# Filter network laid out by feature: VectorE takes relu times decay out of PSUM, no transposes; weights' lower part in one operation, scalars packed

## The chip, the cores and the metric

The kernel runs on one core of one Trainium2 chip. The metric is device time in microseconds (us) of one execution; the median of three runs of the kernel before is 2228.44 us (2227.22 to 2228.93). The five engines work in parallel, each through its own list of instructions in order: TensorE (PE, with its weight loads as PEld), VectorE (DVE), ScalarE (ACT), GpSimd (POOL) and SyncE (SP). SP, ACT and POOL can also issue transfers (DMA); this kernel's loads go out from SP's queue, a few from ACT's. A transfer is carried out by up to 16 DMA engines.

## The reference, cut to what matters

```python
# pos_emb (12480, 64), w1 (64, 64), w2 (64, 128), x and v (2, 12480, 128)
h_mlp = np.maximum(pos_emb @ w1, 0.0) @ w2          # the filter network
window = np.exp(-0.01 * pos)[:, None]               # the decay, positive
h_filt = h_mlp * window
y = irfft(rfft(x * v, 2*S) * rfft(h_filt, 2*S))[:, :S]
x = (x * y).reshape(-1, 128)
h = x @ w_in                                         # w_in (128, 2048), w_out (2048, 128), both float64
g = (a0 + a1*h + a2*h*h + a3*h**3) / (1 + |b0|*|h| + |b1|*h*h + 1e-6)
out = g @ w_out
```

Because the decay is positive, it may stand before the relu, after it, or on the product. In float32 it is zero from position 10398 on, so only the first 82 of 98 blocks of 128 positions carry a filter.

## The kernel before, in words

A position is 128 m + t. The kernel runs in three stretches.

**The first stage** (the loop `for i in range(nb + 2)`, 16 steps of work) computes the filter and prepares weights. A step takes four pairs of residues t, 82 blocks m each, so 328 columns. `load_pos` fetches four rows of `pos_emb` for each m on both sides of the middle (SP, L276, tile `pos`); `hf_w` multiplies them with the decay (DVE, L480 and L486, tile `pw`); `hf_t` turns them to feature-major by four PE transposes (L500) that ACT copies out of PSUM (L503); `hf_1` multiplies with `w1`, placed twice on the diagonal of `bdw1` (PE, L507), and ACT takes the relu out of PSUM (L509, tile `zu`); `hf_2` multiplies with `w2` (PE, L515), and ACT copies the result into `hf` (L521).

Beside it, `weights_gen` turns the float64 words of `w_in` and `w_out` into float32, in 16 pieces of 128 x 256 through tile `raw` (L317, L319). One step of it: DVE takes the two words apart with shifts and masks (L330 to L338) and combines them (L339, tile `f`); POOL adds the two parts (L341); one step later DVE clears what is too small (L346) and ACT scales and rounds (L459, L460 into `win_h`, or L463 into `wout`); a further step later POOL computes the lower part of `w_in` (L455, `win_l`). The steps before the loop's `i = 5` have none of it; 13 pieces are begun in this stage.

Also beside it, POOL multiplies the first 8 of 32 pieces of x and v (L245, `hu`, loaded by L237 and L238 with two buffers each), and DVE computes the scalars of the activation from `a` and `b` in chains of 128 x 1 operations (L361, L364 and others).

**The second stage** (`for g in range(NG + 3)`) does the convolution of the first batch in 32 groups; its first DVE instruction is L563. Each iteration ends with one more x times v on DVE, 24 times, and after those with a remaining step of `weights_gen`.

**The second part** does everything else (second batch, activation, both weight multiplications) and takes most of the time. It comes behind a branch on a computed flag.

All engines follow the order in which the code is written. SP too works in order: a load that waits for a buffer holds up the loads written behind it.

Of the kernel before, what the change touches and what calls it, by code (L numbers as in the profile page):

```python
# [9 lines left out]
F32 = mybir.dt.float32  # L10
# [11 lines left out]
M = 98  # L22
# [40 lines left out]

def constants():
# [31 lines left out]
    win = win.reshape(M, N2)[:96]  # L96
# [14 lines left out]
def build(ctx: ExitStack, tc, x, x_q, v_q, pos_emb, w1, w2, w_in, w_out, moe_a, moe_b,  # L111
# [145 lines left out]
    with ExitStack() as st:  # L257
# [4 lines left out]
        win, bdw1, bdw2 = flat[0][0:96, 0:N2], flat[1][:, 0:128], flat[2][:, 0:2 * D]  # L262
# [5 lines left out]
        NPL = 4  # L268
        pos_t = {}

        def load_pos(p0):
            t = sp.tile([M, 2 * NPL, FO], F32, tag="wa", name="pos", bufs=3)
            for o, t0 in ((0, H2 + p0), (NPL, H2 - p0 - NPL)):
                if MF < M:
                    for r0, r1 in ((0, MF // 16 * 16), (MF // 16 * 16, MF)):
                        nc.sync.dma_start(out=t[r0:r1, o:o + NPL], in_=rows(pos_emb, r0, r1 - r0, t0, NPL, 0, FO))  # L276
                else:
                    load_rows(t[:, o:o + NPL], pos_emb, t0, NPL, 0, FO, True)
            pos_t[p0] = t

        load_pos(0)
        nc.sync.dma_start(out=win, in_=win_d)
        nc.sync.dma_start(out=ident, in_=ident_d)
        load_pos(NPL)
# [38 lines left out]
        def to_f32(raw, n):  # L323
# [4 lines left out]
            fa = sp.tile([128, n], F32, tag="f", name="f", bufs=2)  # L328
# [29 lines left out]

        def ts(o, i, s1, op0, s2=None, op1=None):
            kw = {} if op1 is None else {"op1": op1}  # L360
            nc.vector.tensor_scalar(out=col(o), in0=col(i), scalar1=s1, scalar2=s2, op0=op0, **kw)  # L361

        def tt(o, i, j, op):
            nc.vector.tensor_tensor(out=col(o), in0=col(i), in1=col(j), op=op)  # L364

        def scalars():


            for i in range(4):
                col(f"a{i}")  # L370
            for i in range(2):
                col(f"b{i}")
            nc.scalar.dma_start(out=sc[:, 0:4], in_=moe_a.unsqueeze(0).to_broadcast([128, 4]))
            nc.scalar.dma_start(out=sc[:, 4:6], in_=moe_b.unsqueeze(0).to_broadcast([128, 2]))
            for n in ("a0", "a1", "a2", "a3", "b0", "b1"):
                nc.scalar.activation(out=col("m" + n), in_=col(n), func=AF.Abs)
            tt("sum", "ma0", "ma1", ALU.add)
            tt("sum", "sum", "ma2", ALU.add)
            tt("sum", "sum", "ma3", ALU.add)
            yield  # L380

            ts("d", "ma3", 1e-30, ALU.max)
            nc.vector.reciprocal(out=col("d"), in_=col("d"))
            tt("q", "ma2", "d", ALU.mult)
            tt("q", "q", "ma2", ALU.mult)
            ts("lim", "sum", 16.0, ALU.mult)
            tt("flag", "q", "lim", ALU.is_le)
            ts("q", "ma3", 1024.0, ALU.mult)
            tt("q", "q", "sum", ALU.is_ge)
            yield  # L390
            tt("flag", "flag", "q", ALU.mult)
            ts("q", "mb1", 1e-9, ALU.is_ge)
            tt("flag", "flag", "q", ALU.mult)
            ts("q", "mb1", 1e9, ALU.is_le)
            tt("flag", "flag", "q", ALU.mult)
            tt("q", "mb0", "mb0", ALU.mult)
            ts("lim", "mb1", 16.0, ALU.mult)
            tt("q", "q", "lim", ALU.is_le)
            tt("flag", "flag", "q", ALU.mult)
            yield  # L400
            ts("not", "flag", -1.0, ALU.mult, 1.0, ALU.add)

            tt("b1e", "mb1", "flag", ALU.mult)
            tt("b1e", "b1e", "not", ALU.add)
            tt("a3e", "a3", "flag", ALU.mult)
            tt("a3e", "a3e", "not", ALU.add)
            yield

            for o, i in (("eta", "b1e"), ("sb1", "mb1")):
                ts("d", i, 1e-30, ALU.max)  # L410
                nc.scalar.activation(out=col("d"), in_=col("d"), func=AF.Ln)
                nc.scalar.activation(out=col(o), in_=col("d"), func=AF.Exp, scale=0.5)
                for _ in range(2):
                    nc.vector.reciprocal(out=col("d"), in_=col(o))
                    tt("d", "d", i, ALU.mult)
                    tt("d", "d", o, ALU.add)
                    ts(o, "d", 0.5, ALU.mult)
                yield
# [25 lines left out]
        def weights_gen():  # L444
# [663 lines left out]
```

## Time and profile before

| what | value |
|---|---|
| median of three runs | 2228.44 us |
| the profiled execution's own time | 2228.3 us |
| its span, first to last instruction | 2226.4 us |
| first stage | 0 to 78.6 us |
| second stage | 78.6 to about 357 us |
| DVE busy in the span | 2060.4 us (93%) |
| POOL busy | 2014.7 us (90%) |
| PE busy | 1951.9 us (88%) |
| ACT busy | 1932.1 us (87%) |

Rows of a timeline give start, duration, engine, line, operation, the tiles written and read, and in brackets how long the engine had been idle before and what released it. A line of a helper stands for all who call it. The profiled execution lies within the three runs.

### The profile page before, as it was taken

What the parts mean: (1) busy time and instruction counts of PE and PEld (TensorE: products, weight loads), DVE (VectorE), ACT (ScalarE), POOL (GpSimd) and SP (SyncE); (2) the same over time, 40 slices, a digit from 0 to 9 for tenths busy, and PEclk for the clock granted to TensorE, in tenths of its full rate; (3) what the DMA queues carried; (4) which work ended last, traced back from release to release, by engine and by line L of the source; (5) the groups of instructions that cost most, each with busy time, mean ns of one, the idle gap of its engine ahead of it and who ended that gap; (6) DMA issues with size and microseconds to landing.
All of it is one profiled execution on the core that took longest, in us unless ns stands there. A gap on an engine that the chain in (4) does not pass through costs nothing.

```text
span 2226.4 us, 25191 instructions
## 1 busy us (share of the span) xinstructions
PE 1951.9 (88%) x8352; PEld 1307.8 (59%) x8352; DVE 2060.4 (93%) x2322; ACT 1932.1 (87%) x1971; POOL 2014.7 (90%) x1605
## 2 busy tenths in 40 slices
PE   6899987899999999999999788888888888888886
PEld 4678766566666666666666455445545545545543
DVE  7899995899999998999999889999999999999997
ACT  6422214999999999999999999999999999999997
POOL 5477755999999999999999789999999999999998
PEclk9999988999999999999999999999999999999999
DMA  5344324433143233222222212221122111121100
GB/s 161 108 138 151 120 75 137 118 95 77 39 108 91 51 81 88 74 63 74 56 65 53 49 32 47 48 48 33 31 46 39 38 40 33 48 48 33 36 10 10
DMA packets 148283, 149.61 MB, mean 67 GB/s; under 512 B 88766, under 2 KB 117824, under 8 KB 145264
## 3 DMA queue, kind: packets, MB, share of 16 engines
q1 hardware_dynamic: 141120, 124.16, 22.1%
q10 hardware_dynamic: 7024, 23.76, 3.3%
q8 instruction: 68, 1.11, 0.2%
q14 instruction: 71, 0.58, 0.1%
HBM read 99.72 MB, written 48.17 MB: 66 GB/s over the span
## 4 chain that ended last, share of the span: by engine, by line
POOL 37%; ACT 36%; DVE 10%; PE 9%; issue 5%; DMA 2%; SPq 0%; POOLq 0%; DVEq 0%; ACTq 0%
POOL v L983 18%; POOL v L977 8%; ACT v L912 8%; ACT r L961 8%; ACT l L956 7%; ACT q L940 6%; ACT q L888 5%; POOL q L951 4%; POOL q L950 2%; PE cs L155 2%; PE cs L582 2%; DVE q L967 2%; DVE q L972 1%; ACT q L945 1%; DVE v L922 1%
## 5 line engine op out<-in xcount | busy, mean ns | idle before, releaser
L983 POOL TENSOR_TENSOR v<-v,q 128x970 f32<-128x970 f32 (+3 forms) x416 | 936.3, 2252 | 42.5 <-DVE q L972 40.9
L992 PE MATMUL acc<-v,wout 128*128 128x485 f32 (+3 forms) x1664 | 765.9, 583 | 123.9 <-POOL v L983 116.9
L922 DVE SCALAR_TENSOR_TENSOR v<-v,sc,h 128x970 f32<-128x970 f32 (+3 forms) x416 | 502.9, 1209 | 36.7 <-ACT q L888 32.3
L967 DVE SCALAR_TENSOR_TENSOR q<-q,sc,r 128x970 f32<-128x970 f32 (+3 forms) x416 | 502.6, 1208 | 36.9 <-ACT r L961 34.0
L992 PEld LDWEIGHTS acc<-v,wout 128*128 128x128 f32 x1664 | 293.8, 192 | 377.3 <-POOL v L983 185.0
L972 DVE SCALAR_TENSOR_TENSOR q<-q,r 128x970 f32<-128x970 f32 (+3 forms) x416 | 480.1, 1154 | 13.4
L912 ACT ACTIVATE v<-h,sc 128x970 f32<-128x970 f32 (+3 forms) x416 | 445.3, 1105 | 19.5 <-PE h L880 19.2
L961 ACT ACTIVATE r<-l 128x970 f32<-128x970 f32 (+3 forms) x416 | 426.0, 1024 | 8.7 <-DVE q L972 7.9
L878 PE MATMUL h<-ahi,win_l 128*128 128x486 f32 (+3 forms) x832 | 391.7, 471 | 47.2 <-DVE v L922 45.4
L977 POOL TENSOR_SCALAR v<-v,sc 128x980 f32<-128x980 f32 (+6 forms) x321 | 420.8, 1311 | 0.1
L956 ACT ACTIVATE l<-q,sc 128x1940 f32<-128x1940 f32 (+3 forms) x208 | 405.3, 1949 | 2.2 <-POOL q L951 2.1
L879 PE MATMUL h<-alo,win_h 128*128 128x486 f32 (+3 forms) x832 | 319.3, 384 | 0.0
L888 ACT ACTIVATE q<-h 128x970 f32<-128x970 f32 (+3 forms) x303 | 311.4, 1028 | 8.4 <-PE h L880 8.3
L880 PE MATMUL h<-ahi,win_h 128*128 128x486 f32 (+3 forms) x832 | 317.9, 382 | 0.0
L878 PEld LDWEIGHTS h<-ahi,win_l 128*128 128x128 f32 x832 | 158.2, 190 | 175.7 <-DVE v L922 109.6
L940 ACT ACTIVATE q<-q,sc 128x1940 f32<-128x1940 f32 (+2 forms) x95 | 189.8, 1998 | 0.0
L879 PEld LDWEIGHTS h<-alo,win_h 128*128 128x128 f32 x832 | 158.8, 191 | 35.0 <-issue 19.9
L880 PEld LDWEIGHTS h<-ahi,win_h 128*128 128x128 f32 x832 | 158.3, 190 | 25.7
L945 ACT ACTIVATE q<-q,sc 128x1470 f32<-128x1470 f32 (+3 forms) x113 | 170.9, 1512 | 0.0
L820 PEld LDWEIGHTS cv<-yc,gt 90*98 90x98 f32 x1004 | 118.8, 164 | 31.7 <-DVE an L826 14.4
L820 PE MATMUL cv<-yc,gt 90*98 90x128 f32 x1004 | 128.1, 274 | 7.0 <-DVE an L826 5.6
L951 POOL TENSOR_TENSOR q<-q 128x490 f32<-128x490 f32 (+3 forms) x113 | 111.0, 982 | 9.4
(112 smaller groups left out, 2622.8 us busy)
## 6 DMA issues: line engine op xcount, KB each, us to landing
yc<-y_d SPq DMA_DIRECT2D x23, 900.0 KB
gt<-in_g_dram SPq DMA_DIRECT2D x48, 344.5 KB
xq<-in_x_q_dram SPq DMA_DIRECT2D x64, 196.0 KB
vq<-in_v_q_dram SPq DMA_DIRECT2D x64, 196.0 KB
h_d<-hg ACTq DMA_DIRECT2D x32, 360.0 KB
y_d<-ys ACTq DMA_DIRECT2D x16, 720.0 KB
hg<-h_d SPq DMA_DIRECT2D x64, 180.0 KB
y_d<-ys SPq DMA_DIRECT2D x16, 720.0 KB
```

Of the source, the lines that this page charges most:

```text
L878: nc.tensor.matmul(out=t[:, k, 0:w], lhsT=wl, rhs=hi[:, 0:w], start=True, stop=False)
L879: nc.tensor.matmul(out=t[:, k, 0:w], lhsT=wh, rhs=lo[:, 0:w], start=False, stop=False)
L880: nc.tensor.matmul(out=t[:, k, 0:w], lhsT=wh, rhs=hi[:, 0:w], start=False, stop=True)
L912: nc.scalar.activation(out=v, in_=st_h[s, i], func=AF.Square, bias=col("s"))
L922: stt(out=v, in0=v, scalar=col("k"), in1=h, op0=ALU.add, op1=ALU.mult)
L956: nc.scalar.activation(out=part(st_l, s, i), in_=part(st_q, s, i), func=AF.Ln, **({"bias": col("ka")} if short else {}))
L961: nc.scalar.activation(out=t[:, :, 0:w], in_=halves(st_l[s], i, w), func=AF.Exp, scale=-1.0)
L967: nc.vector.scalar_tensor_tensor(out=q, in0=q, scalar=col("ka") if short else 0.0, in1=st_r[s, i], op0=ALU.add, op1=ALU.mult)
L972: nc.vector.scalar_tensor_tensor(out=q, in0=q, scalar=2.0, in1=st_r.pop((s, i)), op0=ALU.subtract, op1=ALU.mult)
L977: nc.gpsimd.tensor_scalar(out=v, in0=v, scalar1=col("p0" if short else "a0"), scalar2=1.0, op0=ALU.add, op1=ALU.mult)
L983: nc.gpsimd.tensor_tensor(out=v, in0=v, in1=halves(st_q[s], i, w), op=ALU.mult)
L992: nc.tensor.matmul(out=acc[j][:, 0:w], lhsT=wout[:, f, :], rhs=st_v[s][:, i, 0:w], start=(f == 0), stop=(f == NF - 1), skip_group_check=True)
```

## The change

The filter network is laid out by feature. The host passes `pos_q`, in which each step's 128 x 328 input is already feature-major (64 features of the one side of the middle, 64 of the other), so the loads, the multiplication by the decay on DVE and the transposes with their ACT copies go. The decay comes as a second tile of 128 x 328 per step, `win`: two rows of 328 numbers, each of them read for 64 partitions. DVE takes relu times decay out of PSUM in one operation in place of ACT's relu. The unpacking of weights has one operation fewer; the lower part of `w_in` is one DVE operation that also scales, so POOL's subtraction and one of ACT's two operations go; tile `f` has three buffers. The scalars take 39 small DVE operations in place of 65, and their two loads stand first in ACT's queue. `weights_gen` starts at `i = 3` in place of 5, so 14 pieces are begun in the first stage. The identity is loaded late.

```diff
+def by_pair(a):
+    a = np.moveaxis(a[:MF], (0, 1), (-1, -2))
+    a = np.stack([a[..., H2:, :], a[..., H2 - 1::-1, :]])
+    return np.moveaxis(a.reshape(a.shape[:-2] + (H2 // NP, NP * MF)), -2, 0)
...
-        def load_pos(p0):
-            t = sp.tile([M, 2 * NPL, FO], F32, tag="wa", name="pos", bufs=3)
-            for o, t0 in ((0, H2 + p0), (NPL, H2 - p0 - NPL)):
-                if MF < M:
-                    for r0, r1 in ((0, MF // 16 * 16), (MF // 16 * 16, MF)):
-                        nc.sync.dma_start(out=t[r0:r1, o:o + NPL], in_=rows(pos_emb, r0, r1 - r0, t0, NPL, 0, FO))
...
+        def load_pos(i):
+            if i < nb:
+                t = sp.tile([128, W], F32, tag="wa", name="pos", bufs=3)
+                w = sp.tile([128, W], F32, tag="wn", name="win", bufs=3)
+                nc.sync.dma_start(out=t, in_=pos_q[i])
+                nc.sync.dma_start(out=w, in_=win_d[i].unsqueeze(1).to_broadcast([2, FO, W]))
+                pos_t[i] = (t, w)
+
+        nc.scalar.dma_start(out=sc[:, 0:4], in_=moe_a.unsqueeze(0).to_broadcast([128, 4]))
+        nc.scalar.dma_start(out=sc[:, 4:6], in_=moe_b.unsqueeze(0).to_broadcast([128, 2]))
         load_pos(0)
...
+        load_pos(1)
+        load_pos(2)
...
-            fa = sp.tile([128, n], F32, tag="f", name="f", bufs=2)
+            fa = sp.tile([128, n], F32, tag="f", name="f", bufs=3)
...
-            V.tensor_scalar(out=ib, in0=hi, scalar1=signed(0xC0000000), scalar2=None, op0=ALU.bitwise_and)
...
-            V.tensor_tensor(out=ia, in0=ia, in1=ib, op=ALU.bitwise_or)
+            V.scalar_tensor_tensor(out=ia, in0=hi, scalar=signed(0xC0000000), in1=ia, op0=ALU.bitwise_and,
+                                   op1=ALU.bitwise_or)
...
-                        nc.gpsimd.tensor_tensor(out=win_l[:, o], in0=t, in1=win_h[:, o].bitcast(F32), op=ALU.subtract)
+                        nc.vector.scalar_tensor_tensor(out=win_l[:, o], in0=t, scalar=col("eta"),
+                                                       in1=win_h[:, o].bitcast(F32), op0=ALU.mult, op1=ALU.subtract)
...
-                        nc.scalar.activation(out=t, in_=t, func=AF.Identity, scale=col("eta"))
-                        nc.scalar.activation(out=win_h[:, (k - 1) * WN:k * WN], in_=t, func=AF.Identity)
+                        nc.scalar.activation(out=win_h[:, (k - 1) * WN:k * WN], in_=t, func=AF.Identity,
+                                             scale=col("eta"))
...
+        def hf_1(i):
+            t, w = pos_t.pop(i)
             ps = cvs()
+            nc.tensor.matmul(out=ps[:, 1, 0:W], lhsT=bdw1, rhs=t, start=True, stop=True)
             rT[i] = ctile(sp, "zu", 2, CG).rearrange("p r c k -> p (r c k)")[:, 0:W]
-            nc.scalar.activation(out=rT[i], in_=ps[:, 1, 0:W], func=AF.Relu)
+            nc.vector.scalar_tensor_tensor(out=rT[i], in0=ps[:, 1, 0:W], scalar=0.0, in1=w, op0=ALU.max, op1=ALU.mult)
+            load_pos(i + 3)
...
-            for _ in range(2):
-                next(sg, None)
-            if i >= 5:
+            next(sg, None)
+            if i >= 3:
                 next(wg, None)
```

**On DVE, one late step of the first stage** (`pw` is the product with the decay, `raw` the float64 words, `f` and `i_` the unpacking's tiles). Before:

```order
L480 TENSOR_TENSOR pw<-pos,ta_85 82x4x64
L486 TENSOR_TENSOR pw<-pos,ta_85 82x4x64
L346 SCALAR_TENSOR_TENSOR f<-i_634,f 128x256
L330 TENSOR_SCALAR i_678<-raw 128x256
L332 TENSOR_SCALAR i_679<-raw 128x256
L333 TENSOR_SCALAR i_680<-raw 128x256
L335 TENSOR_TENSOR i_678<-i_678,i_679 128x256
L336 TENSOR_SCALAR i_681<-raw 128x256
L338 TENSOR_SCALAR i_679<-i_678 128x256
L339 SCALAR_TENSOR_TENSOR f<-i_680,i_679 128x256
```

and with the change, where `zu` is relu times decay, `cs` PSUM and `win` the decay's tile:

```order
L461 SCALAR_TENSOR_TENSOR zu<-cs,win 128x328
L435 SCALAR_TENSOR_TENSOR win_l<-f,sc,win_h 128x256
L353 SCALAR_TENSOR_TENSOR f<-i_475,f 128x256
L337 TENSOR_SCALAR i_506<-raw 128x256
L339 TENSOR_SCALAR i_508<-raw 128x256
L341 SCALAR_TENSOR_TENSOR i_506<-raw,i_506 128x256
L343 TENSOR_SCALAR i_509<-raw 128x256
L345 TENSOR_SCALAR i_507<-i_506 128x256
L346 SCALAR_TENSOR_TENSOR f<-i_508,i_507 128x256
```

The two products with the decay and one unpacking operation are gone; relu times decay and the lower part have come to DVE.

**On SP, the loads of one step** while x and v are still being loaded. Before:

```order
L317 DMA raw<-in_moe_w_in_dram 128x512
L237 DMA xq<-in_x_q_dram 98x512
L238 DMA vq<-in_v_q_dram 98x512
L276 DMA pos<-in_pos_emb_dram 80x256
L276 DMA pos<-in_pos_emb_dram 2x256
L276 DMA pos<-in_pos_emb_dram 80x256
L276 DMA pos<-in_pos_emb_dram 2x256
```

and with the change:

```order
L324 DMA raw<-in_moe_w_in_dram 128x512
L244 DMA xq<-in_x_q_dram 98x512
L245 DMA vq<-in_v_q_dram 98x512
L283 DMA pos<-in_pos_q_dram 128x328
L284 DMA win<-in_win_dram 128x1x328
```

Four loads of `pos_emb` rows have become one of `pos_q` and one of the decay, in the same place behind x and v; the size printed is that of the tile written, the source of the last one being 2 x 64 x 328.

## Rows read from the trace of the kernel before

**Rows 1.** The page: busy us, share of the span and instructions of each engine.
```profile
PE 1951.9 (88%) x8352; PEld 1307.8 (59%) x8352; DVE 2060.4 (93%) x2322; ACT 1932.1 (87%) x1971; POOL 2014.7 (90%) x1605
```

**Rows 2.** Stretches: window, length, busy PE, PEld, DVE, ACT, POOL, clock, DMA share, GB/s.
```profile
0.00:20.00 20.00, 9.61 (x38) 6.09 (x38) 10.15 (x44) 6.19 (x18) 4.21 (x8) 1.00 0.57 166
...
120.00:140.00 20.00, 20.00 (x110) 16.05 (x109) 19.72 (x29) 5.32 (x10) 16.74 (x17) 1.00 0.54 168
```

**Rows 3.** Timeline of one late step of the first stage, POOL and DVE.
```profile
61.49 0.83 POOL L341 TENSOR_TENSOR f<-f,i 128x256 f32<-128x256 f32 x1 [0.54 <-DVE f L339]
...
61.66 0.94 DVE L486 TENSOR_TENSOR pw<-pos,ta 82x256 f32<-82x256 f32 x1
62.29 2.59 POOL L455 TENSOR_TENSOR win_l<-f,win_h 128x256 fp32r<-128x256 f32 x1
...
64.92 0.42 DVE L339 SCALAR_TENSOR_TENSOR f<-i,i 128x256 f32<-128x256 int32 x1 [0.62 <-POOL win_l L455]
...
65.42 0.83 POOL L341 TENSOR_TENSOR f<-f,i 128x256 f32<-128x256 f32 x1 [0.54 <-DVE f L339]
```

**Rows 4.** Timeline of DVE over the last steps, up to the second stage.
```profile
70.12 0.43 DVE L346 SCALAR_TENSOR_TENSOR f<-i,f 128x256 f32<-128x256 int32 x1 [0.84 <-POOL f L341]
...
73.25 0.43 DVE L346 SCALAR_TENSOR_TENSOR f<-i,f 128x256 f32<-128x256 int32 x1 [0.84 <-POOL f L341]
...
78.27 0.43 DVE L339 SCALAR_TENSOR_TENSOR f<-i,i 128x256 f32<-128x256 int32 x1
78.62 0.90 DVE L563 TENSOR_TENSOR tb<-cs,twh 128x720 f32<-128x720 f32 x1
```

**Rows 5.** Timeline of POOL where it still multiplies x and v.
```profile
31.14 0.84 POOL L341 TENSOR_TENSOR f<-f,i 128x256 f32<-128x256 f32 x1 [6.62 <-DVE f L339]
...
35.44 0.84 POOL L341 TENSOR_TENSOR f<-f,i 128x256 f32<-128x256 f32 x1 [0.36 <-DVE f L339]
```

**Rows 6.** Timeline of DVE at the start.
```profile
7.01 0.22 DVE L547 TENSOR_SCALAR tb<-tb 64x128 f32<-64x128 f32 x1
...
29.18 0.28 DVE L330 TENSOR_SCALAR i<-raw 128x256 int32<-128x256 int32 x1
```

**Rows 7.** Groups by line, 0 to 150 us: count, busy us, mean ns of one.
```profile
L364 DVE TENSOR_TENSOR sc<-sc 128x1 f32<-128x1 f32 x39 | 7.9, 209 | 2.8 <-ACT sc L376 1.7
...
L346 DVE SCALAR_TENSOR_TENSOR f<-i,f 128x256 f32<-128x256 int32 x12 | 5.0, 414 | 2.5 <-POOL f L341 2.5
...
L361 DVE TENSOR_SCALAR sc<-sc 128x1 f32<-128x1 f32 x18 | 2.7, 152 | 0.6
```

**Rows 8.** DMA, 89.5 to 95 us: packets, MB, engines' share; loads in it.
```profile
q1 hardware_dynamic: 224, 0.40, 29.3%
q10 hardware_dynamic: 144, 0.37, 17.8%
...
h_d<-hg ACTq DMA_DIRECT2D x1, 360.0 KB
xq<-in_x_q_dram SPq DMA_DIRECT2D x1, 196.0 KB
vq<-in_v_q_dram SPq DMA_DIRECT2D x1, 196.0 KB
```

**Rows 9.** DMA, 12 to 16 us: the same columns.
```profile
q1 hardware_dynamic: 666, 1.00, 85.3%
```

**Rows 10.** DMA, 0 to 4 us: busy share of the 16 engines in 40 slices.
```profile
DMA  0000000000000000028745222596511355532558
```

**Rows 11.** Timeline of DVE late in the second stage.
```profile
283.33 0.49 DVE L346 SCALAR_TENSOR_TENSOR f<-i,f 128x256 f32<-128x256 int32 x1
...
289.27 0.90 DVE L563 TENSOR_TENSOR tb<-cs,twh 128x720 f32<-128x720 f32 x1
...
320.13 0.91 DVE L563 TENSOR_TENSOR tb<-cs,twh 128x720 f32<-128x720 f32 x1 [0.52 <-POOL zu L180]
...
327.95 0.91 DVE L563 TENSOR_TENSOR tb<-cs,twh 128x720 f32<-128x720 f32 x1 [0.51 <-POOL zu L180]
```

More of the change, by code (lines that the diff above doesn't have):

```diff
@@ L95, in constants @@
     win[:S] = WINDOW
-    win = win.reshape(M, N2)[:96]
+    win = by_pair(win.reshape(M, N2))
     return {
@@ L261, in build @@
         flat = [sp.tile([128, CG * 2 * K1], F32, tag=t, name=t + "0", bufs=2) for t in ("ta", "ta", "tb")]
-        win, bdw1, bdw2 = flat[0][0:96, 0:N2], flat[1][:, 0:128], flat[2][:, 0:2 * D]
+        bdw1, bdw2 = flat[1][:, 0:128], flat[2][:, 0:2 * D]
         twh = sp.tile([N2, 2, 2 * K1], F32, name="twh")
@@ L366, in scalars @@
         def scalars():
[L369 to L377, printed above, removed]
@@ L391, in scalars @@
[L391 to L403, printed above, removed]
@@ L404, in scalars @@
[L404 to L412, printed above, removed]
-                for _ in range(2):
[L414 to L418, printed above, removed]
@@ L431, in scalars @@
[L431 to L442 removed]
+            V = nc.vector
@@ new lines, in scalars @@
+            mul, add, le, ge = ALU.mult, ALU.add, ALU.is_le, ALU.is_ge
+            nc.scalar.activation(out=cols("ma0", "mb1"), in_=cols("a0", "b1"), func=AF.Abs)
+            ts("sum", "ma0", "ma1", add, "ma2", add)
+            ts("lim", "sum", "ma3", add, 16.0, mul)
+            ts("sum", "sum", "ma3", add)
+            ts("d", "ma3", 1e-30, ALU.max)
+            V.reciprocal(out=col("d"), in_=col("d"))
+            ts("q", "ma3", 1024.0, mul, "sum", ge)
+            ts("d", "d", "ma2", mul, "ma2", mul)
@@ new lines, in scalars @@
+            ts("flag", "d", "lim", le, "q", mul)
+            ts("lim", "mb1", 16.0, mul)
+            ts("q", "mb0", "mb0", mul, "lim", le)
+            ts("flag", "mb1", 1e-9, ge, "flag", mul)
+            ts("flag", "mb1", 1e9, le, "flag", mul)
+            ts("flag", "flag", "q", mul)
+            ts("not", "flag", -1.0, mul, 1.0, add)
+            ts("b1e", "mb1", "flag", mul, "not", add)
+            ts("a3e", "a3", "flag", mul, "not", add)
+            i, o, d = cols("mb1", "b1e"), cols("sb1", "eta"), sc[:, 30:32]
@@ new lines, in scalars @@
+            V.tensor_scalar(out=d, in0=i, scalar1=1e-30, scalar2=None, op0=ALU.max)
+            nc.scalar.activation(out=d, in_=d, func=AF.Ln)
+            nc.scalar.activation(out=o, in_=d, func=AF.Exp, scale=0.5)
+            yield
+            for _ in range(2):
+                V.reciprocal(out=d, in_=o)
+                V.tensor_tensor(out=d, in0=d, in1=i, op=mul)
+                V.tensor_tensor(out=d, in0=d, in1=o, op=add)
+                V.tensor_scalar(out=o, in0=d, scalar1=0.5, scalar2=None, op0=mul)
@@ new lines, in scalars @@
+            V.reciprocal(out=cols("ie", "i3"), in_=cols("eta", "a3e"))
+            ts("s", "a2", "eta", mul, "i3", mul)
+            ts("s", "s", 0.5, mul)
+            ts("k", "a1", "b1e", mul, "i3", mul)
+            ts("q", "s", "s", mul)
+            ts("k", "k", "q", ALU.subtract)
+            ts("p0", "a0", "eta", mul, "b1e", mul)
+            ts("p0", "p0", "i3", mul)
+            yield
+            ts("wf", "a3e", "ie", mul, "ie", mul)
+            ts("wf", "wf", "ie", mul, -1.0, mul)
@@ L529, in build @@
         load_u()
-        load_u()
-        for i in range(nb + 2):
+        nc.vector.tensor_scalar(out=bdw2[64:128, D:], in0=bdw2[64:128, D:], scalar1=-1.0, scalar2=None, op0=ALU.mult)
+        for i in range(nb + 1):
             if i < nb:
-                hf_t(i)
-            if 0 <= i - 1 < nb:
-                hf_1(i - 1)
-            if 0 <= i - 2 < nb:
-                hf_2(i - 2)
-            if i == 12:
+                hf_1(i)
+            if i >= 1:
+                hf_2(i - 1)
+            if i == 11:
                 nc.sync.dma_start(out=f1, in_=f1_d)
@@ L545, in build @@
                 nc.sync.dma_start(out=idfth, in_=idfth_d)
-            if i == 0:
-                nc.vector.tensor_scalar(out=bdw2[64:128, D:], in0=bdw2[64:128, D:], scalar1=-1.0, scalar2=None, op0=ALU.mult)
-            for _ in range(2):
-                next(sg, None)
-            if i >= 5:
+                nc.sync.dma_start(out=ident, in_=ident_d)
+            next(sg, None)
+            if i >= 3:
                 next(wg, None)
@@ L1093 @@
     feeds = [("x", inputs["x"]), ("x_q", by_quarter(inputs["x"])), ("v_q", by_quarter(inputs["v"]))]
-    feeds += [(n, inputs[n]) for n in _INS[2:]] + list(constants().items())
+    feeds += [("pos_q", by_feature(inputs["pos_emb"]))] + [(n, inputs[n]) for n in _INS[3:]] + list(constants().items())
     for name, a in feeds:
```

96 lines of the change are left out of this document (19 added, 77 removed).

## The prediction, written before the changed kernel had run

> **What bounds the kernel now.** I began with the page: DVE, POOL, PE and ACT are all busy 87 to 93% [rows 1], which says little, since the change touches only the first 78.6 us and a little of the second stage. So I read the stretches next, then the timeline.
>
> In the first 20 us no engine is busy for more than half the time [rows 2]: the stage starts with waits. DVE does its scalars between the steps, and the first piece of weights is taken up at 29.18 us [rows 6]. From there the pace is that of `weights_gen`. While x and v are multiplied, one addition of POOL follows the other after 4.30 us, 31.14 to 35.44 [rows 5]. Later it is 3.93 us, 61.49 to 65.42 [rows 3]. There the reader is to see a circle: DVE's L339 at 64.92 waits for POOL's `win_l`, whose 2.59 us are long only because DVE works beside it, and POOL's next addition waits for L339. When no `win_l` is left, a step takes 3.13 us, 70.12 to 73.25, of which DVE idles 0.84 us for POOL's addition [rows 4]. DVE then enters the second stage at 78.62 us [rows 4], and there it is the bound: 19.72 us of 20 [rows 2]. What the first stage gains or loses up to 78.62 therefore goes through to the end, since all behind it hangs on DVE's order.
>
> DMA is not the bound now: 166 GB/s at a share of 0.57 [rows 2], with peaks at 85% [rows 9].
>
> **DVE and POOL, if all loads were there in time.** First relu: `bdw2` is scaled at 7.01 us [rows 6]; its load goes out two issues later now, so I put 7.9 us. 39 small operations follow at 0.19 us (between 152 and 209 ns [rows 7]), 7.4 us, and four relus. One relu reads 328 numbers from PSUM. Before shows no such operation; between 414 ns for 256 numbers [rows 7] and 0.90 us for 720 out of PSUM [rows 4] lies 0.49 us, or some 0.42 from start to start. With 0.2 us for ACT's logarithm and exponential the first piece is taken up at 7.9 + 7.4 + 1.7 + 0.2 = 17.2 us, where before had 29.18.
>
> Then 13 steps. Five beside POOL's x times v take 4.3 us each as now (one operation less on DVE, `win_l` more). Four with `win_l` on DVE take 3.2 us, four without it 2.94: the 3.13 us less one operation of 0.2 us, the relu lying in the 0.84 us that DVE idles, since a product that reads PSUM does not stand still for POOL (0.90 us each in the second stage with POOL at work [rows 11]). `win_l` reads two tiles in SBUF, as L486 does, whose 0.94 us beside POOL's addition [rows 3] stand for a wait; hence 3.2 and not 2.9. Sum: 17.2 + 1.35 + 5 x 4.3 + 4 x 3.2 + 4 x 2.94 + 0.35 = 65.0 us to the second stage, 13.6 us early. PE and ACT have less to do than now, and each step leaves them time: ACT four copies and one rounding, PE two products and eight small ones.
>
> **The loads.** Here I expect the other sign. In 89.5 to 95 us three loads ran: x and v, each 98 rows of 2 KB (196 KB), and one transfer of 128 rows (360 KB) on ACT's queue [rows 8]. Queue 1 shows 224 packets. 196 are the rows; 28 are left, 14 for each load. Queue 10 shows 144, that is 128 and 16. I read the extra packets as one closing packet for each DMA engine that took part: 98 rows are dealt to 14 engines, 128 to 16, the largest number up to 16 by which the count divides. The code before cuts 82 rows into 80 and 2, which fits.
>
> The decay's load has a source of 2 rows, each read 64 times, and a target of 128 partitions. The trace has no load whose two sides begin with different counts. If the target's count decides, it goes to 16 engines; if both must divide, to 2. I take 2, since a share of the work has to be a share of both sides' outer counts, and these have only 2 in common. The Trainium skill, page "DMA: Bandwidth & Descriptors", section "Why a DMA increments its semaphore by 16 and not by 1", says that the engines used are the largest number up to 16 that divides the slowest counts of both sides, and that they are the lowest-numbered ones; the extra packets above agree for equal counts, and no row here shows unequal ones. By that rule the load takes 2 engines, always the same two, and the sum is the one that follows; without it, it would be the first rival's.
>
> I further assume that it is always the same two. On two engines each window load is 64 packets of 1312 bytes, 84 KB, on each of them. And since every other load of SP's queue also has a part on these two, behind whatever was issued before, all loads of the stage come at the pace of these two. Up to the last of the 16 windows each carries 16 x 84 KB = 1.344 MB of decay, 16 x 8 x 1312 bytes = 0.168 MB of `pos`, 20 loads of x and v with 7 rows of 2 KB = 0.287 MB, 11 pieces of `raw` with 16 KB = 0.180 MB, and 0.025 MB of constants: 2.00 MB.
>
> What does one engine move? In 12 to 16 us, all crowded, 1.00 MB took 85.3% of 16 engines [rows 9], 54.6 us of engine time: 18.3 GB/s. The quiet transfer of queue 10 took 17.8% of 16 engines over 5.5 us, 15.7 us for 0.37 MB [rows 8]: 23.6 GB/s. The two engines will not share with fourteen busy ones, so I go near the upper, 22 GB/s; 18.3 and 23.6 are the ends. 2.00 MB then take 91.0 us (109.3; 84.7). Bytes begin to move at 1.7 us [rows 10], so the last window lands at 92.7 us. Does the queue run dry? No: three windows are ahead, each 3.8 us on the two engines, and SP is held up behind x and v only for a multiplication of POOL.
>
> Behind the last window still stand: its next piece of `raw` 0.7 us, taking it up 1.35, two more steps of 2.94, 0.35 to the second stage, together 8.3 us. Second stage at 101.0 us: 22.4 us late. Most of DVE's work of 65.0 us lies inside the waits and counts no more.
>
> **The second stage.** An iteration with a step of weights took from 283.33 to 289.27 us on top of the rest; 5.94 us, against which a plain iteration of 7.82 (320.13 to 327.95) has 0.52 us of idling [rows 11], so 5.3 us in all. One of three such steps now lies in the first stage: 5.3 us less. The remaining two have one operation fewer: 0.5 us. Together 5.8 us (5 to 7).
>
> **Sum.** 22.4 - 5.8 = 16.6 us more. From the profiled execution's 2228.3 us, which is the median within 0.2, that makes 2245 us. With 23.6 GB/s and 7 us it is 2237, with 18.3 GB/s and 5 us 2264.
>
> **The rivals.**
> - The window load goes to 16 engines, or to two that change from load to load, so that windows travel side by side. Then a step's loads (336 KB of `pos` and `win`, 262 KB of `raw`, 401 KB of x and v: 1.0 MB) take 4.0 us at the 250 GB/s of [rows 9] (1.00 MB in 4 us) against a step of 4.3, DVE and POOL set the pace, and 13.6 + 5.8 us are gained: 2209 us. For it: the target has 128 rows, and all large loads here use 14 or 16. Against it: the source's count. It decides if a window load is closed by 16 packets, or if two windows land close together.
> - Two engines, but quick enough to be hidden. No change needs the second stage at 84.4 us, so 2.00 MB in 74.4 us, 26.9 GB/s each; no row shows that. It would give 2228 us.
> - Two engines, and slower than the crowded ones, as in the short bursts of queue 1 in [rows 8]: 29.3% of 16 engines over 5.5 us, 25.8 us for 0.40 MB, 15.5 GB/s. 2.00 MB take 129 us, the time is 2283 us.
> - A smaller gain: loads in time, but DVE and POOL stay in step at 3.9 us as now, because `win_l` on DVE stands still for POOL: 8 steps x 0.85 = 6.8 us less gain, 2216 us.
>
> A rule that speaks on the last one stands in the Trainium skill, page "SBUF — State Buffer", section "Who interferes with whom": a DVE operation with two SBUF inputs and a POOL operation that reads SBUF exclude each other for a whole operation, and one with at most one SBUF input does not contend. L486's 0.94 us agree. By it `win_l` waits and the relu does not, as priced above, and the sum stays.
>
> **How the numbers follow.** Forecast 0.80, 16 engines with the full gain 0.09, smaller gain 0.03, hidden 0.04, slower than crowded 0.04. The time is the forecast's, 2245 us; the range takes its own ends, 2236 to 2264, and leaves out some 0.2. Runs of this kernel lie within 0.1% of each other, and 0.2%, 4.5 us, is about what tells a change from none: faster 0.13, same 0.04, slower 0.83.
>
> **What would show it.** Right: in the first stage DVE stands before the relu for `win` and before the unpacking for `raw`; a window comes about every 5 to 6 us; the share of the DMA engines stays low while loads are outstanding; first product with `twh` near 101 us; two steps of weights in the second stage. Wrong: first product near 65 us and DVE hardly waiting for loads; or windows coming every 4.3 us or quicker.

## The result, and the profile after

The changed kernel takes 2241.65 us in the median of six runs (2240.47 to 2243.09), the kernel before 2228.68 in six (2227.22 to 2229.12): a ratio of 1.0058, 95% interval [1.0047, 1.0068]. It is slower, by 13.0 us; the forecast was 2245. In the profiled executions the span went from 2226.4 to 2239.5 us, 13.1 more. The first product with `twh`, which opens the second stage, came 22.44 us later (101.06 against 78.62 [rows 4]). The second stage, first to last such product, took 8.66 us less (248.50 against 257.16), and what lies behind it 0.7 us less. 22.44 - 8.66 - 0.7 = 13.1. One of the four runs of the changed kernel of experiment 5 was slow, at a granted clock of 0.914, and is left out of the time given there.

The page of the changed kernel, its row of busy time:

```profile
PE 1949.2 (87%) x8288; PEld 1301.9 (58%) x8288; DVE 2048.3 (91%) x2272; ACT 1918.6 (86%) x1924; POOL 1991.8 (89%) x1597
```

Every engine has less to do than in [rows 1], DVE by 12 us, and the kernel is slower all the same. Stretches of the changed kernel (window, length, busy PE, PEld, DVE, ACT, POOL, clock, DMA share, GB/s):

```profile
0.00:20.00 20.00, 3.49 (x7) 1.82 (x8) 1.64 (x9) 1.49 (x2) 1.67 (x6) 1.00 0.44 127
...
80.00:100.00 20.00, 13.89 (x46) 8.52 (x47) 11.69 (x38) 9.91 (x21) 3.62 (x5) 0.83 0.48 144
```

In the first 20 us DVE works 1.64 us where it worked 10.15 [rows 2], and 80 us later it still idles for eight of 20. The waits of DVE from 0 to 105 us say for what (us in total, times, longest):

```profile
DVE tb L481 <- DMA tb<-in_w_dram: 18.2, 1, 18.2
DVE i L337 <- DMA raw<-in_moe_w_in_dram: 16.9, 6, 4.3
DVE i L337 <- DMA raw<-in_moe_w_out_dram: 7.3, 4, 2.7
DVE zu L461 <- DMA win<-in_win_dram: 3.1, 2, 1.8
```

45.5 us of waiting for loads. Most of it is not booked under the decay's own load, which is the slow one, but under others: `raw`, which stands behind it in SP's queue, and `w2` (tile `tb`), which comes from ACT's queue. The DMA view from 65 to 80 us shows the slow one at work (busy share of the 16 engines in tenths, and GB/s, in 40 slices):

```profile
DMA  1115887831111111167995111111118499611111
GB/s 52 51 46 94 165 295 274 310 139 58 49 49 49 49 49 49 56 191 175 333 358 188 45 49 45 49 45 49 48 49 124 166 383 331 230 53 49 49 49 49
```

Over half of the time the share stands at one tenth and the rate at 49 GB/s, between bursts of 200 to 380. Each plateau follows the issue of a window's load (by SP's timeline at 67.20, 71.71 and 76.57), so 2 of 16 engines carry it, at 24.5 GB/s each. Whether it is always the same two shows at the start. Three windows are issued by 6.2 us, the last two shown here; then SP's queue (q1) from 0 to 7.2 us and from 7.2 to 9.6 us (packets, MB, share of 16 engines):

```profile
2.43 0.59 SPq L284 DMA_DIRECT2D win<-in_win_dram  x1
...
5.68 0.54 SPq L284 DMA_DIRECT2D win<-in_win_dram  x1
```

```profile
q1 hardware_dynamic: 498, 0.60, 31.9%
```

```profile
q1 hardware_dynamic: 95, 0.12, 13.4%
```

Three windows and three `pos` are 1.01 MB, and nothing else stands in SP's queue before 8.76 us. At 7.2 us 0.41 MB are left, more than two windows, and still the share is 13.4%, two engines, at 50 GB/s. With another pair for each window it would be about twice that. Last, DVE's timeline at the start, at the end of the first stage, and late in the second:

```profile
18.23 0.23 DVE L481 TENSOR_SCALAR tb<-tb 64x128 f32<-64x128 f32 x1 [18.23 <-DMA tb<-in_w_dram]
...
28.10 0.58 DVE L337 TENSOR_SCALAR i<-raw 128x256 int32<-128x256 int32 x1
...
93.50 0.29 DVE L337 TENSOR_SCALAR i<-raw 128x256 int32<-128x256 int32 x1 [1.68 <-DMA raw<-in_moe_w_out_dram]
...
95.19 0.49 DVE L461 SCALAR_TENSOR_TENSOR zu<-cs,win 128x328 f32<-128x328 f32 x1
96.11 0.42 DVE L353 SCALAR_TENSOR_TENSOR f<-i,f 128x256 f32<-128x256 int32 x1 [0.43 <-POOL f L348]
...
99.04 0.42 DVE L353 SCALAR_TENSOR_TENSOR f<-i,f 128x256 f32<-128x256 int32 x1 [0.84 <-POOL f L348]
...
101.06 0.90 DVE L510 TENSOR_TENSOR tb<-cs,twh 128x720 f32<-128x720 f32 x1
...
298.23 0.90 DVE L510 TENSOR_TENSOR tb<-cs,twh 128x720 f32<-128x720 f32 x1
311.11 0.90 DVE L510 TENSOR_TENSOR tb<-cs,twh 128x720 f32<-128x720 f32 x1
318.72 0.90 DVE L510 TENSOR_TENSOR tb<-cs,twh 128x720 f32<-128x720 f32 x1
326.17 0.91 DVE L510 TENSOR_TENSOR tb<-cs,twh 128x720 f32<-128x720 f32 x1 [0.15 <-POOL zu L187]
```

The scaling of `bdw2` waits until 18.23 (7.01 in [rows 6]); the last wait for a load ends at 93.50; from there on only POOL's addition is waited for, and a step takes 2.93 us (96.11 to 99.04; 3.13 in [rows 4]). Over the stage the relus, one for each window, come 5.3 us apart (31.34 to 95.19, twelve steps): the sign of 5 to 6 us was right.

### The profile page after: what moved, and what is told of

It reads as the page before. It is cut to its first block, busy times and chain, and to the rows that moved or that the text cites. A ratio compares the mean times of both kernels' runs of the same rounds, so it can differ in the third digit from the quotient of the medians.

```text
span 2239.5 us, 24919 instructions
## 1 busy us (share of the span) xinstructions
PE 1949.2 (87%) x8288; PEld 1301.9 (58%) x8288; DVE 2048.3 (91%) x2272; ACT 1918.6 (86%) x1924; POOL 1991.8 (89%) x1597
## 4 chain that ended last, share of the span: by engine, by line
ACT 36%; POOL 34%; DVE 12%; PE 8%; issue 5%; DMA 5%; SPq 0%; POOLq 0%; DVEq 0%; ACTq 0%
POOL v L930 17%; ACT v L859 8%; ACT r L908 8%; POOL v L924 8%; ACT l L903 7%; ACT q L887 6%; ACT q L835 5%; POOL q L898 3%; DVE q L914 3%; PE cs L162 2%; DVE q L919 2%; POOL q L897 2%; DVE v L869 2%; ACT q L892 2%; PE cs L529 2%
## 5 line engine op out<-in xcount | busy, mean ns | idle before, releaser
L919 DVE SCALAR_TENSOR_TENSOR q<-q,r 128x970 f32<-128x970 f32 (+3 forms) x416 | 480.0, 1154 | 13.4
```

The costliest lines, as they stand in the source:

```text
L919: nc.vector.scalar_tensor_tensor(out=q, in0=q, scalar=2.0, in1=st_r.pop((s, i)), op0=ALU.subtract, op1=ALU.mult)
```

## The experiments

Theory A: the decay's load runs on 2 of 16 DMA engines because its source has an outer count of 2, and these two set the pace of the first stage. Rivals: it is something else in the new loads or in their queue (order, one queue, a late start), or in the new DVE work. All kernels compute everything. Times in us are medians; ratios are to the kernel before, run on the same chip beside them (its median lay between 2228.97 and 2231.35, so ratios compare better than times between groups).

**1. The same bytes to the same 128 partitions in two loads of 64**, so that the outer count on both sides is 64:

```diff
-                nc.sync.dma_start(out=w, in_=win_d[i].unsqueeze(1).to_broadcast([2, FO, W]))
+                for h in range(2):
+                    nc.sync.dma_start(out=w[FO * h:FO * h + FO], in_=win_d[i, h].unsqueeze(0).to_broadcast([FO, W]))
```

> The decay is loaded by two transfers per step, each of 64 partitions from one row read 64 times, so that the source begins with a count of 64 in place of 2; bytes, tiles and all else as in the changed kernel. Theory A (the load with a source of 2 rows runs on 2 DMA engines, always the same, and everything behind it on SP's queue comes at their pace): the first stage falls to the pace of DVE and POOL, second stage entered at 65 to 68 us in place of 101, time 2209 to 2213 us. Rival B (64 reads of the same row are slow in themselves, or the 2.6 MB more of loads): still entered later than 90 us, time above 2230. Rival C (DVE and POOL hold each other up so much that the loads only cover it): entered at 75 to 80 us, time 2220 to 2225.

Measured: 2208.26, ratio 0.9905 [0.9889, 0.9922]. First `twh` product at 69.33. That is theory A, a little outside both of its ranges: 1.3 us behind the one for the product, 0.7 us under the one for the time. DVE's waits for loads from 0 to 80 us, in the kernel of the halves:

```profile
DVE tb L482 <- DMA tb<-in_w_dram: 9.7, 1, 9.7
...
DVE i L338 <- DMA raw<-in_moe_w_in_dram: 1.8, 3, 1.0
```

Of 45.5 us of waits 11.5 are left, and 33 us of time are gone with one line. From 20 to 50 us its DMA view gives

```profile
DMA  9999999999999999999999999999999899999989
...
q1 hardware_dynamic: 5014, 7.13, 99.3%
```

99.3% of 16 engines, 239 GB/s: no plateau of two engines is left. The rows are still read 64 times each, so that was not what cost the 33 us; the number by which the transfer is dealt out was.

**2 and 3. The source with 4 rows, or with 16**, each read 32 or 8 times in one load:

```diff
-    win = by_pair(win.reshape(M, N2))
+    win = np.repeat(by_pair(win.reshape(M, N2)), 2, axis=1)
...
-                nc.sync.dma_start(out=w, in_=win_d[i].unsqueeze(1).to_broadcast([2, FO, W]))
+                nc.sync.dma_start(out=w, in_=win_d[i].unsqueeze(1).to_broadcast([4, 32, W]))
```

(with 16: `np.repeat` by 8 and `[16, 8, W]`).

> The same single load per step, but its source has 4 rows (each of the 2 stored twice), each read for 32 partitions. Theory A: 4 engines, each with 0.67 MB of windows and 0.66 MB of the rest, 1.33 MB; at the 24.5 GB/s that two engines show in the changed kernel (49 GB/s at a share of 0.125) 54 us, so the last window lands near 57 us and the loads are nearly hidden: second stage at 66 to 72 us, time 2210 to 2216. Rival B (reads of the same row, or the bytes): as the changed kernel, above 2235.

> The same single load per step with a source of 16 rows, each read for 8 partitions. Theory A: 16 engines, 0.83 MB on each, 34 us, no bound: the same time as with two halves, 2209 to 2213, and DVE hardly waits for loads. Rival B: between the changed kernel and before, since each row is read less often, but not at the time of the halves.

Measured: four rows 2219.91, ratio 0.9958 [0.9944, 0.9972], first `twh` at 78.81; sixteen 2211.21, 0.9918 [0.9901, 0.9934], first `twh` at 69.83. So 2, 4 and 16 rows give 101.1, 78.8 and 69.8 us: the first stage goes with the source's outer count, and with 16 it ends within 0.5 us of that of the halves (the whole kernel takes 3 us more than the halves; the rest of that is not explained). Four rows missed their expected time: beside the waits for `raw` (6.6 us) the start is late too, `bdw2` at 14.7 us against 9.7 in the halves, which I had not priced. But their number of engines can be read: from 57.0 to 59.3 us, behind a window issued at 55.12, SP's queue shows

```profile
q1 hardware_dynamic: 185, 0.22, 26.6%
```

that is about four engines, at 95 GB/s together. And with sixteen rows, from 20 to 50 us:

```profile
q1 hardware_dynamic: 4568, 6.72, 76.8%
```

Nearly the bytes of the halves (7.13 MB) at a share of 76.8%, not 99.3%: the two loads of 64 keep the engines busy longer for the same bytes. Behind the start DVE waits 1.8 us for loads in the one and 0.8 in the other, so it costs little here; why it is so was not tried.

**4. The load of two rows unchanged, but on ACT's queue:**

```diff
-                nc.sync.dma_start(out=w, in_=win_d[i].unsqueeze(1).to_broadcast([2, FO, W]))
+                nc.scalar.dma_start(out=w, in_=win_d[i].unsqueeze(1).to_broadcast([2, FO, W]))
```

> The load with 2 rows unchanged, but issued on ACT's queue, so that other loads of SP's queue are not behind it in the same queue. Theory A with the two engines as the bound: the two engines still have 2.00 MB to move up to the last window, some 82 us at 24.5 GB/s, so the second stage is entered at 85 to 97 us, time 2225 to 2238; raw, x and v come earlier than in the changed kernel and DVE's waits move from raw to win. Rival D (it is only the order in SP's queue that holds up the other loads, two engines would do): entered before 75 us, time under 2220.

Measured: 2239.84, ratio 1.0047 [1.0031, 1.0064], first `twh` at 98.60. That it is only the order on one queue falls; but the gain that theory A gave it was too large as well. The waits are shared out otherwise and are about as long together, 45.9 us:

```profile
DVE i L337 <- DMA raw<-in_moe_w_in_dram: 14.0, 4, 5.7
DVE zu L461 <- DMA win<-in_win_dram: 13.9, 7, 4.5
DVE tb L481 <- DMA tb<-in_w_dram: 13.1, 1, 13.1
DVE i L337 <- DMA raw<-in_moe_w_out_dram: 4.9, 3, 2.3
```

Another queue does not help a load that shares its DMA engines.

**5. The loads of `w1` and `w2` ahead of all others**, in the changed kernel and in that of the halves:

```diff
-        load_pos(0)
...
-            nc.scalar.dma_start(out=bdw1[64 * i:64 * i + 64, 64 * i:64 * i + 64], in_=w1)
+            nc.sync.dma_start(out=bdw1[64 * i:64 * i + 64, 64 * i:64 * i + 64], in_=w1)
...
-            nc.scalar.dma_start(out=bdw2[64 * i:64 * i + 64, :].rearrange("p (s c) -> p s c", s=2),
+            nc.sync.dma_start(out=bdw2[64 * i:64 * i + 64, :].rearrange("p (s c) -> p s c", s=2),
...
+        load_pos(0)
```

> The changed kernel, its window load with the source of two rows as it is, but with the loads of w1 and w2 issued on SP's queue ahead of the first pos and window. Nothing is left out. It tells what the late start of the changed kernel was worth: bdw2 was scaled at 18.23 us where the sum had 7.9. Theory: the two engines set the pace, and a start 10 us earlier only moves the waits behind it: the scaling comes at 5 to 7 us, but the first twh product stays at 95 to 101 and the time is 2236 to 2242, at most 5 us less. Rival: the two engines idled while the stage waited for w2, so the whole 10 us come through: first twh product near 91, time 2231 to 2233.

> The kernel of the halves with the loads of w1 and w2 issued on SP's queue ahead of the first pos and window, not on ACT's queue beside them. Nothing is left out. In the halves bdw2 is scaled at 9.75 us and the first piece of weights is taken up at 19.44; before had the scaling at 7.01. Theory: the small loads come late because the large ones issued beside them fill the engines first; issued first, they land by 6 to 7 us, the first piece is taken up at 16 to 17, and the start of the second stage moves from 69.3 to 66 or 67: time 2205 to 2206. Rival: the first product does not wait for w2 but for the first pos and window, which now land later by what the small loads take; then the scaling is early but the first relu is not, the second stage starts within 1 us of 69.3 and the time is 2208.

Measured, changed kernel: 2242.69 in the median of three runs, ratio 1.0057 [1.0037, 1.0077]; first `twh` at 103.64. The scaling came at 5.41 us instead of 18.23, and nothing was gained: the waits moved as the theory said, but product and time lie behind its ranges. Its waits:

```profile
DVE zu L461 <- DMA win<-in_win_dram: 17.3, 5, 6.7
DVE i L337 <- DMA raw<-in_moe_w_in_dram: 16.9, 6, 4.8
DVE i L337 <- DMA raw<-in_moe_w_out_dram: 7.4, 4, 2.9
DVE tb L481 <- DMA tb<-in_w_dram: 5.4, 1, 5.4
```

13 us of waiting for `w2` became 14 us of waiting for `win`, 47.0 us in all: the sum of waits is set by the transfer, the name on a wait by the order. In the kernel of the halves: ratio 0.9921 [0.9904, 0.9937], scaling at 5.19, first `twh` at 69.23 against 69.33; there the theory fell and its rival held. The first relu then waited 2.38 us for its product, and the later loads came no earlier.

**6. The lower part of `w_in` on POOL again**, in the kernel of the halves:

```diff
-                        nc.vector.scalar_tensor_tensor(out=win_l[:, o], in0=t, scalar=col("eta"),
-                                                       in1=win_h[:, o].bitcast(F32), op0=ALU.mult, op1=ALU.subtract)
+                        nc.gpsimd.tensor_tensor(out=win_l[:, o], in0=t, in1=win_h[:, o].bitcast(F32), op=ALU.subtract)
...
-                        nc.scalar.activation(out=win_h[:, (k - 1) * WN:k * WN], in_=t, func=AF.Identity,
-                                             scale=col("eta"))
+                        nc.scalar.activation(out=t, in_=t, func=AF.Identity, scale=col("eta"))
+                        nc.scalar.activation(out=win_h[:, (k - 1) * WN:k * WN], in_=t, func=AF.Identity)
```

> The kernel of the halves with one part of the change undone: the lower part of w_in is again a subtraction on POOL behind two operations of ACT, not one operation on DVE. Nothing is left out. Theory: what moving it to DVE gained is the circle of the later steps, in which DVE's L339 waited for POOL's subtraction of 2.59 us [rows 3]: the four steps with a lower part and no x times v go from 3.1 back to some 3.9 us, 3.2 us in all; the five beside x times v stay at 4.3, since POOL's adding sets them, or grow by up to 0.3 each because POOL has more to do. First twh product at 72.5 to 74, time 2211 to 2213. Rival: POOL's subtraction finds room now that the relu is out of ACT and DVE does less: no change, 2208, or the sum is worse since POOL's x times v fall behind in all nine steps: above 2215.

Measured: 2212.28, ratio 0.9918 [0.9902, 0.9935], first `twh` at 69.61: 0.3 us later than in the first profile of the halves (69.33), 1.9 later than in the second (67.69, below). The theory's 3.2 us were too much; between the rest and the rival's "no change" this does not decide, since the ratios' intervals (0.9905 for the halves) overlap. Its timeline, one late step:

```profile
47.42 0.72 POOL L349 TENSOR_TENSOR f<-f,i 128x256 f32<-128x256 f32 x1 [2.10 <-DVE f L347]
48.10 0.73 POOL L436 TENSOR_TENSOR win_l<-f,win_h 128x256 fp32r<-128x256 f32 x1
48.18 0.93 DVE L354 SCALAR_TENSOR_TENSOR f<-i,f 128x256 f32<-128x256 int32 x1 [0.49 <-POOL f L349]
...
50.93 0.72 POOL L349 TENSOR_TENSOR f<-f,i 128x256 f32<-128x256 f32 x1 [2.10 <-DVE f L347]
```

POOL's subtraction now takes 0.73 us, not the 2.59 of [rows 3]. The difference is who began. Here it begins 0.08 us ahead of DVE's L354, which then takes 0.93 us instead of some 0.42. In the kernel before it begins at 62.29, while DVE is at work on the product with the decay; DVE goes on without a pause up to 64.29, through these operations and those between them,

```profile
62.53 0.41 DVE L346 SCALAR_TENSOR_TENSOR f<-i,f 128x256 f32<-128x256 int32 x1
...
64.01 0.28 DVE L338 TENSOR_SCALAR i<-i 128x256 int32<-128x256 int32 x1
```

and the subtraction ends at 64.88, 0.59 us behind the last of them. The step takes 3.51 us (before 3.93); with the subtraction on DVE, in the halves, it takes 3.10 (51.74 to 54.84 below) where `raw` is there in time, 1.6 us less in four steps; but in the first profile of the halves two of the four waited for `raw` (0.95 and 0.45 us), which gave most of it back. In the kernel of the halves:

```profile
51.34 0.49 DVE L462 SCALAR_TENSOR_TENSOR zu<-cs,win 128x328 f32<-128x328 f32 x1
51.56 0.73 POOL L349 TENSOR_TENSOR f<-f,i 128x256 f32<-128x256 f32 x1 [2.90 <-DVE f L347]
51.74 0.82 DVE L436 SCALAR_TENSOR_TENSOR win_l<-f,sc,win_h 128x256 fp32r<-128x256 f32 x1
52.49 0.41 DVE L354 SCALAR_TENSOR_TENSOR f<-i,f 128x256 f32<-128x256 int32 x1
...
54.84 0.83 DVE L436 SCALAR_TENSOR_TENSOR win_l<-f,sc,win_h 128x256 fp32r<-128x256 f32 x1
```

The relu beside POOL's addition takes its 0.49 us; `win_l`, which is shorter by a fifth (256 numbers for 328) but reads two tiles of SBUF, takes 0.82. L354, as long as `win_l` and with two tiles of SBUF too, takes 0.41 right behind it, when POOL's addition is over (52.29). The Trainium skill, page "SBUF — State Buffer", section "Who interferes with whom", separates just these two kinds by the number of SBUF inputs; these rows agree.

**7. The old filter network, with the new weights and scalars.** The kernel before, with everything of the change but the layout by feature; weights begun as early as in the change:

```diff
-            for _ in range(2):
-                next(sg, None)
-            if i >= 5:
+            next(sg, None)
+            if i >= 4:
```

(and the packed scalars, the unpacking with one operation fewer, and `win_l` on DVE as in the change).

> The kernel of before with only the weights' and scalars' parts of the change: the lower part in one operation on DVE, one operation fewer in the unpacking, the packed scalars, with the old filter network (transposes, decay ahead of them). The weights begin one product earlier than before, so that two steps lie in the second stage. Nothing is left out. It shares out the gain of the halves (2208.3 against 2228.7 us). Theory: of 20.4 us, 8.7 are the second stage's (one step fewer there and one operation fewer in the rest) and come here too; the scalars and the shorter steps give the first stage some 4 to 6 us; the rest, 6 to 8 us, was the two multiplications by the decay and the transposes, which stay here. Time 2214 to 2217. Rival: the old network alone set the start (first piece at 29.18 us, behind the transposes' loads), so that only the second stage's 8.7 are seen: 2219 to 2221. Or the network costs nothing beside the weights: 2208 to 2210.

Measured: ratio 0.9926 [0.9909, 0.9943], first `twh` at 71.80, second stage 248.65. The time (2214.43) lies in the theory's range, but not for its reasons: in the first stage the scalars and weights bring 6.8 us (78.62 to 71.80), though one more step of weights lies in it, where 4 to 6 were expected, and the new network only 2.5 (71.80 against 69.33; 4.1 against the second profile of the halves), where 6 to 8 were.

**8 and 9. A step of weights more, or none, in the second stage**, in the kernel of the halves. One more:

```diff
-            if i >= 3:
+            if i >= 4:
                 next(wg, None)
```

None, by two more steps at the end of the first stage:

```diff
             if i >= 3:
                 next(wg, None)
+            if i >= nb - 1:
+                next(wg, None)
```

> The kernel of the halves with the weights begun one product later in the first stage (i of 4 on, not 3), so that three steps of weights lie in the second stage, as before the change, and not two. Nothing is left out. The second stage of the changed kernel lost 8.7 us against before where the sum said 5.8. Theory: one step of weights there costs not 5.3 us but some 8, because the iteration that follows two or three of them finds the granted clock of TensorE lower and waits for its products (before: an iteration of 9.9 us without a step of weights, where the changed kernel has 7.6). Then the first stage ends 2.9 us earlier than in the halves (first twh product near 66.4), the second stage takes 256 to 257 us instead of 248.5, and the time is some 5.3 us more than the halves' 2208.3, near 2213.5. Rival: a step costs the 5.3 us of the sum and the rest of the 8.7 came from the operation less in each of the others: then the second stage takes some 253.7 us and the time is near 2210.6. For the document's own sum either way the first stage and the second are to be read apart.

> The kernel of the halves with the last two steps of weights taken in the first stage too, at its last two iterations, so that none with unpacking is left in the second. Nothing is left out. Theory: a step costs 2.94 us at the end of the first stage and 5.0 in the second (iterations of 12.87 against 7.88), where it also lowers TensorE's granted clock in the iteration behind it. First twh product 5.9 us later, near 75.2; second stage 248.5 - 2 x 5.0 + 0.3 to 0.6 = 239 us; the time 3 to 4 us less than the halves run beside it. Rival: the last loads of weights do not come in time (DMA share 0.76 in 50 to 60 us), so that the two steps wait 1 to 2 us each: no difference, within 1 us of the halves.

> The kernel of the halves unchanged, on the same chip as the one without late steps, so that a few us between them can be told. Nothing is left out. Expected as in its first run: ratio to before 0.9905 within 0.0017, first twh product at 69.3, second stage 248.5 us.

Measured, one more: ratio 0.9935 [0.9918, 0.9951]; first `twh` at 66.84, second stage 255.27, that is 6.8 us for the step, between theory (8) and rival (5.3). Two stretches of that kernel, the third step's iteration and the one behind it, which unpacks nothing:

```profile
277.00:289.80 12.80, 9.64 (x50) 7.12 (x48) 12.66 (x18) 1.61 (x4) 7.02 (x7) 1.00 0.04 16
289.80:298.60 8.80, 4.70 (x25) 4.70 (x26) 7.63 (x12) 2.15 (x5) 3.62 (x5) 0.61 0.40 126
```

and the same two of the kernel before:

```profile
289.30:302.40 13.10, 9.06 (x48) 6.76 (x46) 12.89 (x19) 2.05 (x5) 6.88 (x7) 1.00 0.03 11
302.40:312.30 9.90, 5.83 (x25) 5.80 (x26) 7.60 (x12) 1.94 (x4) 4.75 (x6) 0.66 0.32 101
```

In the second and third long iteration PE is busy 9 to 10 us of 13 (in the first some 12); in the one behind three of them its granted clock is 0.61 and 0.66, the iteration takes 8.8 and 9.9 us. In the changed kernel, with two, it takes 7.61 (311.11 to 318.72) at a clock of 1.00:

```profile
298.20:311.10 12.90, 8.81 (x42) 7.82 (x43) 12.76 (x18) 3.14 (x6) 7.02 (x7) 0.87 0.35 116
311.10:318.70 7.60, 6.25 (x39) 5.21 (x39) 7.49 (x12) 1.08 (x2) 2.47 (x4) 1.00 0.00 0
```

That the clock is what DVE pays for shows in PE's and DVE's rows of the kernel before in that iteration, with one stretch of it,

```profile
306.47 3.69 PE L582 MATMUL cs<-idfth,yy 128*90 128x128 f32 x16 [6.88 <-DVE zh L571]
312.30 0.91 DVE L563 TENSOR_TENSOR tb<-cs,twh 128x720 f32<-128x720 f32 x1 [2.20 <-POOL yy L209]
```

```profile
306.40:308.40 2.00, 1.93 (x9) 1.96 (x10) 2.00 (x3) 0.00 (x0) 0.18 (x1) 0.50 0.00 0
```

and the same 16 products in the changed kernel:

```profile
311.82 1.91 PE L529 MATMUL cs<-idfth,yy 128*90 128x128 f32 x16
```

PE had idled 6.88 us for DVE. Its next 16 products ran at a granted clock of 0.50, the lower level of 1.2 GHz, in 3.69 us instead of 1.91, and the eight behind them in 2.26 instead of 1.49. PE's products, not POOL's `yy` (done at 311.81), end last before DVE's wait of 2.20 us is over, at 312.21.

Measured, none: 2204.00 (2202.37 to 2205.11), ratio 0.9889 [0.9872, 0.9905]; the halves beside it 2207.77 (2206.95 to 2208.73), 0.9905 [0.9889, 0.9922]. First `twh` 5.89 us later than in the halves of the same group (73.58 and 67.69), second stage 9.99 shorter (238.52 and 248.51); 3.8 us of time are gained, as expected, and the four runs of the one all lie below the four of the other. (The halves' own first stage ended 1.6 us earlier than in their first profile, where `raw` was waited for twice as long.) With no long iteration left, PE's same 16 products take 1.91 to 1.95 us throughout. It is the fastest version here, 1.1% below the kernel before.

## Why the prediction was right

Point by point, by its own steps.

- **The loads.** *I take 2* [engines] was right, and so was *always the same two*. The two are shown by the plateau of 49 GB/s and by 2, 4 and 16 rows in experiments 1 to 3, the same two by the start, where more than two windows share them. The Trainium skill, page "DMA: Bandwidth & Descriptors", section "Why a DMA increments its semaphore by 16 and not by 1", gives the largest number up to 16 that divides both sides' slowest counts; for counts of 2 against 128 this case now shows it, and in experiment 1 an outer step of length zero counts as any other.
- **The rate.** 22 GB/s for each engine was a choice between 18.3 and 23.6. Alone the two move 24.5, above the upper end. Over the whole stage 22 holds: from 3.6 to 93.5 us the DMA share never falls below a tenth, so at no time are fewer than two engines at work, and the last wait for a load ends at 93.50 us where 92.7 + 0.7 = 93.4 was forecast. That it is met within 0.1 us is luck in part; what the two carry while the other fourteen are busy was not measured by itself.
- **The start.** `bdw2` was put at 7.9 us and came at 18.23; the first piece of weights at 28.10 instead of 17.2. This cost nothing, since *most of DVE's work of 65.0 us lies inside the waits*: experiment 5 mended the first and gained nothing. In the halves they come at 9.75 and 19.44, the first piece 2.2 us late. (A small slip of reading: DVE is busy 10.15 of the first 20 us in [rows 2], a little over half.)
- **Behind the last load**: 7.58 us forecast from the piece of `raw`, 7.56 measured; the second stage at 101.0 and at 101.06. In detail the last wait was for `raw`, not for the window, whose relu at 95.19 no longer waited.
- **Steps without loads in the way.** 4.3, 3.2 and 2.94 us were forecast; the halves show 4.29 (three steps from 29.08 to 41.96), 3.10 and 2.93. The relu out of PSUM takes 0.49 us as bounded. It is not the loads that set the 4.3, though the DMA engines are at 99.3% there: with sixteen rows, at 76.8% and with no wait for a load in these steps, a step takes 4.14 (30.72 to 43.15, three steps). In both DVE's L354 (L353 with sixteen rows) takes 1.48 us in each of them, beside POOL's 1.45 for x times v, and 0.41 in the later ones: DVE itself stands for POOL, and 3.10 + 1.07 = 4.17.
- **The second stage** is the term that was mis-sized: 5.8 us forecast, up to 7 in the range, 8.66 measured. The step fewer was put at 5.3 us (the working as written, 5.94 less 0.52, gives 5.4); 13.13 against 7.88 gives 5.25, and 13.13 against 12.87 another 0.26 for the operation fewer in each of two others: these parts were right. Left out was what three long iterations do to the one behind them: 9.90 before, 7.61 after, 2.3 us, in which TensorE's clock is 0.66 before and 1.00 after. Experiments 8 and 9 show a third step at 6.8 us and the first two at 5.0 each. Of the remaining 0.6 us, 0.45 lie in the two iterations behind it (7.45 and 7.74 against 7.82).
- **The rivals.** The first, 16 engines, was priced at 2209 us; with 16 engines experiment 1 takes 2208.3 and experiment 3 2211.2. So the sign hung on the one question of how the load is dealt out. But that the rival's sum came out is luck in part: its first stage gained 9.3 us (69.33), not 13.6 (65.0), 2.2 of it missing at the start and 1.8 in waits for `raw`, and its second stage 8.6, not 5.8.

## What to carry to other kernels

Before a load with a broadcast source, look at the outer count of both its sides: this one lost 33 us, 1.5% of the kernel, to a source written as 2 x 64 instead of twice 64. When waits for loads appear, look at the share of the DMA engines while something is outstanding and not at the name on the wait; issuing the waited-for load sooner or on another queue only moved the name here. And place work by what it costs in each stage, with the clock of the iteration behind it in the price: a step of weights costs 2.94 us in the first stage and 5.0 to 6.8 in the second.

## What the runs showed of the hardware

Two DMA engines with packets of 1312 bytes moved 24.5 GB/s each when the other fourteen rested, and four 24 each. With all at work a busy engine moved 239 / 16 = 15 GB/s in the halves, at a share of 99.3%, and 18 with sixteen rows (225 GB/s at 76.8%); so the lower rate goes with the kind of load too, not with the crowd alone. POOL's subtraction of 256 columns took 2.59 us where DVE was at work first, and ended 0.59 us behind the last of DVE's operations; it took 0.73 us in experiment 6, where it began first, and then DVE's operation was the long one. By this it was the neighbour, not the operation, that made it long. And 16 products of PE took 3.69 us at a granted clock of 0.50, behind an idle stretch of 6.88 us, and 1.91 at 1.00.
